# Second mixture of a fused attention and two-mixture kernel: router rounds cut into pieces, quarter additions reordered, one weight sum moved

## The chip, the cores and the metric

One core of a Trainium2 chip runs the whole kernel. The metric is the device time of one execution in microseconds (us). The kernel before took 1454.73 us, the median of 3 runs (1454.37 to 1455.91).

## The reference

Attention over clusters, then a gated feed-forward block, then a second mixture of eight experts whose weights per token come from a router that is balanced in eight rounds. Only the second mixture (`_moe2_ref`) is touched:

```python
N, D = x.shape                      # 1536 tokens, 512
E = w_gate.shape[1]                 # 8 experts, F = 1024
logits = x @ w_gate
logits = logits - logits.max()
P = np.exp(logits)
for _ in range(8):
    P /= P.sum(1, keepdims=True) + 1e-09
    P /= P.sum(0, keepdims=True) + 1e-09
    P *= N / E
out = np.zeros((N, D), dtype=np.float32)
for e in range(E):
    h = np.maximum(x @ w1[e], 0.0)
    ye = h @ w2[e]
    out += P[:, e:e + 1] * ye
```

## The kernel before

The second mixture is done in 16 sets (`s`), each half an expert's 1024 hidden columns. A set is two matrix products, each by the fast scheme that takes seven block products in place of eight, so it has 14 products, `i` = 0 to 13; `n` = 14 s + i. Products 0 to 6 make the hidden layer (PSUM tiles `a`), 7 to 13 the output layer (tiles `b`). Each float32 product is three matmuls of halves: a high part (`wfh`, `ah`, `xfh`, cast by ScalarE, written ACT below) and a low part (`wfl`, `al`, `xfl`, the difference, taken by VectorE, DVE). One block product of a layer is itself done by seven quarter products: `quad(s, q)` computes one into PSUM tile `q` (first layer's products 0 to 2) or `r` (`four=True`, for product 7), and `quad_add` lets DVE add it into the hidden block `h`. Quarters 1, 6, 7 and 4 share one PSUM bank (`QB`), so each waits until the one before it is added.

All four compute engines run an order that is written out by hand in one loop over `n`: what is written earlier is earlier on its engine's queue, and an instruction that waits holds up all behind it on that engine. At the top of a step come the operands for products one to three ahead (`factor` is `factor_hi` on ACT and `factor_lo` on DVE; `h_hi` and `h_lo` the same for hidden blocks; `h_s1` to `h_s4` sum hidden blocks on DVE) and the emptying of the product just done (`evacuate_a`, `evacuate_b`); then the matmuls of product `i`. In the output layer the products 1, 6, 7 and 4 (steps 7, 9, 11, 13) accumulate in one set of three PSUM banks, with a read by `evacuate_b` between them; the staging buffer of each read is a quarter of `acc1` (`RING` for the first seven).

`gate()` is a generator that computes the router's weights `Pg` on the side. The table `ROUNDS` says how many of its pieces are run at the end of which step (s, i). A round has two pieces: nine DVE instructions on the 128x12x8 weights, and one matmul `col` of the column sums `cs` against ones, which TensorE (PE) runs in its own order. Its results are first read when expert 1 starts (set 2, step 8). `w_t4` subtracts a weight sum in place (`ws`) for product 13 at step 11, just ahead of the cast of that sum. `x4_sums` and `x4_rest` make operands of the quarters of product 7 from the `x` that lies in `acc1`; set 0, steps 11 to 13, and set 1, products 1 and 2, hold them.

The lines of the profile that the prediction speaks of: L652 and L1041 are the products' matmuls, L1021 the quarters, L991 `col`, L747 DVE's sums (quarter additions are `h<-q` and `h<-r`), L750 its low parts, L1174 `h_s2`, L1074 and L1072 ACT's casts of hidden blocks, L863 its casts of weights, L1137, L1130 and L1116 the emptying of output products (ACT with weights, ACT without, DVE in the last set), L983 to L995 the router's rounds.

Of the kernel before, what the change touches and what calls it, by code (L numbers as in the profile page):

```python
# [8 lines left out]
F32 = mybir.dt.float32  # L9
# [8 lines left out]
P = 128  # L18
# [7 lines left out]
E = 8  # L26
# [12 lines left out]
def attention_moe_kernel(ctx, tc, kq, vp, cent, w_in, w_out, w_gate, w1, w2, out):  # L39
# [706 lines left out]
    def tt(e, out, in0, in1, op):  # L746
        e.tensor_tensor(out=out, in0=in0, in1=in1, op=op)  # L747
# [84 lines left out]
    def w_t4(n, e):  # L832
        _, _, b21, _, t = wst[n // 7]
        tt(e, t, b21, t, ALU.subtract)
# [105 lines left out]
    def gate():  # L940

        pair = ahp.tile([P, HT], F32, name="pair", tag="ah")
        first, lt = pair[:, :CH], pair[:, CH:]
        gps.memset(first[: P // 2], 0.0)
        ps = ps1.tile([P, 512], F32, name="gl", tag="g")[:, :CH]

        def logits(k0):
            for k in (k0, k0 + 1):
                for c in range(4):
                    nc.tensor.matmul(ps[CQ * c : CQ * (c + 1)], lhsT=wgr[:, k], rhs=acc1[:, k, c * CH : (c + 1) * CH], start=k == 0, stop=k == KC - 1, skip_group_check=True)  # L950

        logits(0)
        yield
        act.copy(first[P // 2 :], ps[: P // 2])
        yield
        logits(2)
        yield
        tt(vec, lt, ps, first, ALU.add)
        for _ in range(2):
            yield  # L960
        plog = ps1.tile([P, 512], F32, name="plog", tag="g")
        for t in range(CH // P):
            nc.tensor.transpose(plog[:, t * P : (t + 1) * P], lt[:, t * P : (t + 1) * P], ident)
        act.copy(Pg.rearrange("p (c t) e -> p c t e", c=4), plog[:, :CH].rearrange("p (t c x) -> p c t x", t=CH // P, c=4)[:, :, :, :E])
        mx = sk.tile([P, 4], F32, name="mx")
        vec.tensor_reduce(out=mx[:, 0:1], in_=Pg, axis=AX.XY, op=ALU.max)
        yield
        yield
        ps = ps1.tile([P, 512], F32, name="mxt", tag="g")
        nc.tensor.transpose(ps[:1, :P], mx[:, 0:1], ident)  # L970
        vec.tensor_reduce(out=mx[:1, 1:2], in_=ps[:1, :P], axis=AX.X, op=ALU.max, negate=True)
        yield
        yield
        ps = ps1.tile([P, 512], F32, name="mxb", tag="g")
        nc.tensor.matmul(ps[:, :1], lhsT=ones[:1, :], rhs=mx[:1, 1:2], start=True, stop=True)
        vec.tensor_copy(mx[:, 2:3], ps[:, :1])
        yield
        act.activation(Pg, Pg, AF.Exp, bias=mx[:, 2:3])
        rs = sk.tile([P, TT], F32, name="rs")
        cs = sk.tile([P, E], F32, name="cs")  # L980
        cr = sk.tile([P, E], F32, name="ccr")
        for it in range(8):
            vec.tensor_reduce(out=rs, in_=Pg, axis=AX.X, op=ALU.add)  # L983
            vec.tensor_scalar(out=rs, in0=rs, scalar1=1e-9, scalar2=None, op0=ALU.add)
            vec.reciprocal(rs, rs)
            tt(vec, Pg, Pg, rs.unsqueeze(2).to_broadcast([P, TT, E]), ALU.mult)
            vec.tensor_reduce(out=cs, in_=Pg.rearrange("p t e -> p e t"), axis=AX.X, op=ALU.add)
            yield
            yield
            ps = ps1.tile([P, 512], F32, name=f"col{it}", tag="g")  # L990
            nc.tensor.matmul(ps[:, :E], lhsT=ones, rhs=cs, start=True, stop=True)  # L991
            vec.tensor_scalar(out=cr, in0=ps[:, :E], scalar1=1e-9, scalar2=None, op0=ALU.add)
            vec.reciprocal(cr, cr)
            tt(vec, Pg, Pg, cr.unsqueeze(1).to_broadcast([P, TT, E]), ALU.mult)
            vec.tensor_scalar(out=Pg, in0=Pg, scalar1=float(NTOK // E), scalar2=None, op0=ALU.mult)  # L995


    sets = {}

# [95 lines left out]
        return to[i * HT : (i + 1) * HT, j * HD : (j + 1) * HD].rearrange("(t p) d -> p t d", p=P)  # L1095

    stages, stores = [0], [0]
    RING = (0, 1, 0, 1, 2, 0, 1)
    kept = {}

    def stage():
# [213 lines left out]
    nc.sync.dma_start(out=wgr[:, :, :E], in_=w_gate.rearrange("(k p) e -> p k e", p=P))  # L1315
    ones = sk.tile([P, P], F32, name="ones")
    gps.memset(ones, 1.0)
    Pg = sk.tile([P, TT, E], F32, name="Pg")

    gating = None  # L1320
    LATES = {7: 6, 8: 3, 9: 7, 10: 2, 11: 4}
    ROUNDS = {**{(0, i): 1 for i in range(14)}, (1, 2): 1, (1, 3): 2, (1, 4): 1, **{(1, i): 1 for i in range(10, 14)}, (2, 2): 1, (2, 3): 2, (2, 4): 2}
    acc2 = acc1.rearrange("p k (t d) -> p k t d", d=HD)
    ENG = mybir.EngineType
    with tc.manual_schedule(engines={ENG.PE, ENG.DVE, ENG.Activation, ENG.Pool}):
        psn = {}
        for n in range(14 * NS + 1):
# [3 lines left out]
            if late:  # L1331
                h_hi(s, late, 1, late == 2)
                h_lo(s, late, 1, late == 2)
            if i == 5:
                factor_hi(n + 3)
                if s == 0:
                    h_hi(s, 1, 0, relu=True)
                    h_hi(s, 1, 1, relu=True)
# [8 lines left out]
            if i == 0:  # L1347
                if s == 0:
                    x_quad_rest(2, 4)
                    t2 = h_block(0, "21")  # L1350
                    x_sum(t2, (1, 1), (0, 1))
                    x_factor(6, t2)
                else:
                    quad_factor(s)
                    factor(n + 2, vec)
                    w_sums2(n, vec)
                factor(n + 3, vec)
# [11 lines left out]
            if i == 3:  # L1369
                factor(n + 2, vec)  # L1370
                factor(n + 3, vec)
                if s:
                    quad_factor(s, True)
                w_load(n + 11)
                if s == 0:
                    x_sum((1, 0), (1, 0), t2)
                    x4_raw()
# [41 lines left out]
            if i in (8, 9):  # L1419
                factor(n + 2, vec)  # L1420
            if i in (10, 11, 12, 13):
                if i == 11:
                    w_t4(n - 4, vec)
                if i == 12:
                    w_load(n + 9)
                    w_sums1(n + 2, vec)
                factor(n + 2, vec)
                if i == 13:
                    quad_sums(s + 1)
                if s == 0:  # L1430
                    if i == 11:
                        x4_sums()
                    if i > 11:
                        x4_rest(i - 12)
            p = order(n)[i % 7]
            if i == 0:
                g = groups1(n, ready.pop(n), xf[1])
# [6 lines left out]
            elif i == 1:  # L1444
# [4 lines left out]
                multiply(psn[n + 1], g[1:2], False)  # L1449
                quad_add(s, 5)  # L1450
                quad_add(s, 6)
                if s == 1:
                    x4_rest(2)
                if s == 0:
                    x_sum((0, 0), t2, (0, 0), (0,))
            elif i == 2:
# [2 lines left out]
                quad(s, 3)  # L1459
                multiply(psn[n], g[3:], False)  # L1460
                quad_add(s, 7)
                if s == 1:
                    x4_rest(3)
                if s == 0:
                    x_sum((0, 0), t2, (0, 0), (1,))
                quad(s, 4)
                quad_add(s, 3)
                if s == 0:
                    x_factor(7, (0, 0), (0,))
                quad_add(s, 4)  # L1470
# [6 lines left out]
            elif i == 6:  # L1477
                if s == 0:
                    psn[n] = whole4(s, n)
            elif i < 7:  # L1480
                psn[n] = product(n, groups1(n, ready.pop(n), xf[p]))
            elif i == 7 and s:
                for q in (2, 1, 5):
                    quad(s, q, True)
                g = groups2([hf.pop((s, p, k)) for k in range(2)], ready.pop(n))
                psn[n] = sets[n // 7, 1] = [ps3.tile([P, 512], F32, name=f"b{s}_1_{u}", tag="s") for u in range(3)]
                opened = set()
                half_product(psn[n], g, 0, slice(0, 6), opened)
                quad_add(s, 2, True)
                quad_add(s, 1, True)  # L1490
                quad_add(s, 5, True)
                h_s1(s, (1,))
                h_hi(s, 5, 1)
                quad(s, 6, True)
                quad(s, 3, True)
                half_product(psn[n], g, 1, slice(0, 3), opened)
                quad_add(s, 6, True)
                h_lo(s, 5, 0)
                factor(n + 2, vec)
                quad_add(s, 3, True)  # L1500
                quad(s, 7, True)
                half_product(psn[n], g, 1, slice(3, 6), opened)
                quad_add(s, 7, True)
                h_lo(s, 5, 1)
                quad(s, 4, True)
                ready.pop(n - 1)
                h_s2(s, (0,))
                h_hi(s, 6, 0)
                quad_add(s, 4, True)
                h_s2(s, (1,))  # L1510
                h_lo(s, 6, 0)
            else:
                psn[n] = product(n, groups2([hf.pop((s, p, k)) for k in range(2)], ready.pop(n)), by_half=n < 14 * NS - 1)
            psn.pop(n - 3, None)
            if n == 0:
                gating = gate()
            if gating is not None:
                if s == 2 and i == 7:
                    for _ in gating:
                        pass  # L1520
                for _ in range(ROUNDS.get((s, i), 0)):
                    next(gating, None)


_OUTS = [((NTOK, DM), 'float32')]
# [35 lines left out]
```

## Time and profile before

| | |
|---|---|
| profiled execution, own time | 1453.9 us |
| its span, first to last instruction | 1452.1 us |
| median of 3 runs | 1454.73 us (1454.37 to 1455.91) |
| PE busy | 1432.2 us (99%) |
| DVE busy | 1207.1 us (83%) |
| ACT busy | 965.3 us (66%) |
| POOL busy | 367.3 us (25%) |
| granted clock of PE | 1.00 |
| span of the second mixture | from 486.5 us on |

The own time lies 1.8 us above the span and 0.8 us below the median of the runs. PE is busy in nearly all of the span, so time can be won only where its matmuls start later than the ones before them allow; the rows below show such places. A set takes 59.0 us.

### The profile page before, as it was taken

What the parts mean: (1) busy time and instruction counts of PE and PEld (TensorE: products, weight loads), DVE (VectorE), ACT (ScalarE), POOL (GpSimd) and SP (SyncE); (2) the same over time, 40 slices, a digit from 0 to 9 for tenths busy, and PEclk for the clock granted to TensorE, in tenths of its full rate; (3) what the DMA queues carried; (4) which work ended last, traced back from release to release, by engine and by line L of the source; (5) the groups of instructions that cost most, each with busy time, mean ns of one, the idle gap of its engine ahead of it and who ended that gap; (6) DMA issues with size and microseconds to landing.
All of it is one profiled execution on the core that took longest, in us unless ns stands there. A gap on an engine that the chain in (4) does not pass through costs nothing.

```text
span 1452.1 us, 25386 instructions
## 1 busy us (share of the span) xinstructions
PE 1432.2 (99%) x9703; PEld 1290.1 (89%) x9704; DVE 1207.1 (83%) x2045; ACT 965.3 (66%) x1848; POOL 367.3 (25%) x356
## 2 busy tenths in 40 slices
PE   8999999999999999999999999999999999999998
PEld 5777777888888898989999999999999999999997
DVE  7788888778787989997888878888788787887888
ACT  7677677654735476648767577676775876757764
POOL 6677653111120000201332222120211211202111
PEclk9999999999999999999999999999999999999999
DMA  7665621121130026657598797785956959659576
GB/s 211 183 178 147 183 65 45 58 73 59 58 102 29 3 95 144 111 100 175 114 199 131 145 192 119 155 133 94 196 93 118 159 88 176 112 100 181 87 147 131
DMA packets 136315, 177.49 MB, mean 122 GB/s; under 512 B 6273, under 2 KB 108673, under 8 KB 136193
## 3 DMA queue, kind: packets, MB, share of 16 engines
q0 software_dynamic: 83584, 87.30, 39.7%
q1 hardware_dynamic: 51104, 87.32, 19.5%
q8 instruction: 76, 1.25, 0.3%
q10 hardware_dynamic: 1504, 1.25, 0.3%
q14 instruction: 47, 0.38, 0.1%
HBM read 65.36 MB, written 88.87 MB: 106 GB/s over the span
## 4 chain that ended last, share of the span: by engine, by line
PE 71%; DVE 7%; ACT 3%; issue 2%; DVEq 0%; ACTq 0%
PE b L652 27%; PE a L652 20%; PE y L706 9%; PE q L1021 4%; PE b L1041 4%; PE r L1021 3%; PE l L652 3%; DVE h L747 1%; DVE wfl L750 1%; DVE acc L1116 1%; ACT h L674 1%; DVE h L678 1%; ACT acc L1137 0%; ACT gh L688 0%; ACT h L683 0%
## 5 line engine op out<-in xcount | busy, mean ns | idle before, releaser
L652 PE MATMUL b<-wfh,ah 128*128 128x256 f32 x1164 | 332.9, 286 | 2.8 <-DVE acc L1116 2.0
L652 PE MATMUL b<-wfl,ah 128*128 128x256 f32 x1164 | 329.1, 283 | 0.0
L652 PE MATMUL b<-wfh,al 128*128 128x256 f32 x1164 | 329.1, 283 | 0.0
L1146 POOL DMA_DIRECT2D out_dram<-acc x87 | 126.5, 1712 | 557.6 <-ACT acc L1137 460.5
L652 PEld LDWEIGHTS b<-wfh,ah 128*128 128x128 f32 x1164 | 222.7, 191 | 7.8 <-DVE h L747 2.9
L652 PEld LDWEIGHTS b<-wfl,ah 128*128 128x128 f32 x1164 | 222.9, 192 | 0.0
L652 PEld LDWEIGHTS b<-wfh,al 128*128 128x128 f32 x1164 | 222.9, 192 | 0.0
L652 PE MATMUL a<-xfh,wfh 128*128 128x512 f32 (+1 forms) x640 | 215.9, 337 | 0.1
L652 PE MATMUL a<-xfl,wfh 128*128 128x512 f32 (+1 forms) x640 | 215.8, 337 | 0.0
L652 PE MATMUL a<-xfh,wfl 128*128 128x512 f32 (+1 forms) x640 | 215.5, 337 | 0.0
L1074 ACT CAST ah<-h 128x768 fp32r<-128x768 f32 x160 | 135.1, 845 | 117.8 <-DVE h L1174 54.8
L1137 ACT ACTIVATE acc<-b,Pg 128x256 f32<-128x256 f32 x512 | 198.6, 505 | 0.0
L1061 ACT COPY h<-a 128x512 f32<-128x512 f32 x192 | 111.7, 603 | 109.5 <-PE a L652 99.7
L750 DVE TENSOR_TENSOR al<-h,ah 128x768 fp32r<-128x768 f32 x160 | 152.7, 955 | 11.0 <-ACT ah L1074 6.5
L652 PEld LDWEIGHTS a<-xfh,wfl 128*128 128x128 f32 x640 | 120.9, 189 | 12.9
L652 PEld LDWEIGHTS a<-xfh,wfh 128*128 128x128 f32 x640 | 121.1, 189 | 11.8 <-issue 0.6
L652 PEld LDWEIGHTS a<-xfl,wfh 128*128 128x128 f32 x640 | 121.1, 189 | 10.3
L313 ACT ACTIVATE p<-s,m 128x768 f32<-128x768 f32 x96 | 86.5, 902 | 39.5 <-DVE m L304 36.9
L304 DVE TENSOR_REDUCE m<-s 128x1 f32<-128x768 f32 x96 | 90.0, 951 | 13.5 <-PE s L297 13.1
L323 POOL TENSOR_SCALAR p<-p,rec 128x768 f32<-128x768 f32 x96 | 86.4, 912 | 49.1 <-DVE rec L318 40.1
L747 DVE TENSOR_TENSOR h<-q,h 128x384 f32<-128x384 f32 x112 | 61.9, 556 | 40.7 <-PE q L1021 38.7
L111 POOL TENSOR_TENSOR wr<-wr,u 128x512 f32<-128x512 f32 x32 | 44.2, 1383 | 183.2 <-DVE u L110 146.3
(260 smaller groups left out, 3402.6 us busy)
## 6 DMA issues: line engine op xcount, KB each, us to landing
out_dram<-acc POOLq DMA_DIRECT2D x91, 768.0 KB, 9.3
w0r<-in_w_dram SPq DMA_DIRECT2D x16, 1024.0 KB, 5.6
w1r<-in_w_dram SPq DMA_DIRECT2D x16, 1024.0 KB, 7.2
qk<-qk SPq DMA_DIRECT2D x45, 192.0 KB, 3.5
wr<-in_w_in_dram SPq DMA_DIRECT2D x16, 512.0 KB, 3.8
wr<-in_w_out_dram SPq DMA_DIRECT2D x16, 512.0 KB, 3.5
first_out<-acc POOLq DMA_DIRECT2D x10, 768.0 KB, 9.2
raw<-in_kq_dram SPq DMA_DIRECT2D x16, 384.0 KB, 4.4
```

What stands on the lines that cost most here:

```text
L304: nc.vector.tensor_reduce(out=m, in_=tiles[i]["s"][:, :S], axis=AX.X, op=ALU.max, negate=True)
L313: nc.scalar.activation(t["p"], t.pop("s")[:, :S], AF.Exp, bias=t.pop("m"), accum_out=chunks[c]["sum"][:, j, 0:1])
L323: nc.gpsimd.tensor_scalar(out=p, in0=p, scalar1=chunks[c]["rec"][:, j : j + 1], scalar2=1.0, op0=ALU.mult, op1=ALU.mult)
L652: nc.tensor.matmul(ps[u][:, cols], lhsT=lf(i, k), rhs=rt(j, k), start=fresh and u not in opened, stop=k == 1 and q == 2, skip_group_check= ...
L706: nc.tensor.matmul(out, lhsT=w[:, k, d * P : (d + 1) * P], rhs=g, start=first, stop=last, skip_group_check=True)
L747: e.tensor_tensor(out=out, in0=in0, in1=in1, op=op)
L750: e.tensor_tensor(out=lo, in0=x, in1=r(hi), op=ALU.subtract)
L1021: nc.tensor.matmul(ps, lhsT=quad_lhs(s, q, a, four), rhs=(x4 if four else xq)[b][:, XQ[q]], start=j == 0 and q in (1, 2, 5), stop=j == 2, ...
L1061: act.copy(bank(t, u), ps[u])
L1074: act.copy(hi, x)
L1137: act.mul(t[:, 2 * u + m], z[:, m], g)
L1146: gps.dma_start(out=to, in_=t, accum_op=ALU.add)
```

## The change

Six things. The router's weights lie in a tile with a ninth column that always holds 1e-9, so the row sums come out with that addend, and the factor N / E is part of the column factor: seven DVE instructions in a round in place of nine. A round has four pieces, and the pieces are spread anew: some between the quarter additions of products 1 and 2 of sets 1 and 2, three at a time at the top of steps 10 and 12 of set 1. In product 7 the last quarter's addition comes ahead of both `h_s2`, and the low part of the next weights after the addition of quarter 7. `w_t4` moves from step 11 to the top of step 10. `x4_sums` moves from step 11 to 12 of set 0, the four parts of `x4_rest` to set 0 step 13 (two), set 1 step 0 and step 3. In `RING` the fifth and sixth staging buffers change places.

```diff
         for it in range(8):
             vec.tensor_reduce(out=rs, in_=Pg, axis=AX.X, op=ALU.add)
-            vec.tensor_scalar(out=rs, in0=rs, scalar1=1e-9, scalar2=None, op0=ALU.add)
             vec.reciprocal(rs, rs)
-            tt(vec, Pg, Pg, rs.unsqueeze(2).to_broadcast([P, TT, E]), ALU.mult)
-            vec.tensor_reduce(out=cs, in_=Pg.rearrange("p t e -> p e t"), axis=AX.X, op=ALU.add)
-            yield
+            if it:
+                yield
+            tt(vec, shares, shares, rs.unsqueeze(2).to_broadcast([P, TT, E]), ALU.mult)
+            vec.tensor_reduce(out=cs, in_=shares.rearrange("p t e -> p e t"), axis=AX.X, op=ALU.add)
             yield
             ps = ps1.tile([P, 512], F32, name=f"col{it}", tag="g")
             nc.tensor.matmul(ps[:, :E], lhsT=ones, rhs=cs, start=True, stop=True)
-            vec.tensor_scalar(out=cr, in0=ps[:, :E], scalar1=1e-9, scalar2=None, op0=ALU.add)
+            yield
+            vec.tensor_scalar(out=cr, in0=ps[:, :E], scalar1=1e-9, scalar2=float(E / NTOK), op0=ALU.add, op1=ALU.mult)
             vec.reciprocal(cr, cr)
-            tt(vec, Pg, Pg, cr.unsqueeze(1).to_broadcast([P, TT, E]), ALU.mult)
-            vec.tensor_scalar(out=Pg, in0=Pg, scalar1=float(NTOK // E), scalar2=None, op0=ALU.mult)
-
+            tt(vec, shares, shares, cr.unsqueeze(1).to_broadcast([P, TT, E]), ALU.mult)
+            yield
+
+    def route(times):
+        for _ in range(times):
+            next(gating)
...
-    RING = (0, 1, 0, 1, 2, 0, 1)
+    RING = (0, 1, 0, 1, 0, 2, 1)
...
-    Pg = sk.tile([P, TT, E], F32, name="Pg")
+    Pg = sk.tile([P, TT, E + 1], F32, name="Pg")
+    shares = Pg[:, :, :E]
+    gps.memset(Pg, 1e-9)
...
-    ROUNDS = {**{(0, i): 1 for i in range(14)}, (1, 2): 1, (1, 3): 2, (1, 4): 1, **{(1, i): 1 for i in range(10, 14)}, (2, 2): 1, (2, 3): 2, (2, 4): 2}
+    ROUNDS = {**{(0, i): 1 for i in range(12)}, (0, 12): 3, (0, 13): 1, (1, 2): 1, (1, 3): 3, (1, 4): 1, (1, 10): 1, (1, 12): 1, (2, 2): 1, (2, 3): 3, (2, 4): 1, (2, 5): 1}
...
             if late:
                 h_hi(s, late, 1, late == 2)
                 h_lo(s, late, 1, late == 2)
+            if i == 10:
+                w_t4(n - 3, vec)
+            if s == 1 and i in (10, 12):
+                route(3)
...
-                if i == 11:
-                    w_t4(n - 4, vec)
...
-                if s == 0:
-                    if i == 11:
-                        x4_sums()
-                    if i > 11:
-                        x4_rest(i - 12)
+                if s == 0 and i == 12:
+                    x4_sums()
+                if s == 0 and i == 13:
+                    x4_rest(0, 1)
...
                 quad_add(s, 7)
-                if s == 1:
-                    x4_rest(3)
+                if 0 < s < 3:
+                    route(1)
...
                 quad_add(s, 3)
+                if 0 < s < 3:
+                    route(1)
...
                 quad_add(s, 6, True)
                 h_lo(s, 5, 0)
-                factor(n + 2, vec)
+                factor_hi(n + 2)
                 quad_add(s, 3, True)
                 quad(s, 7, True)
                 half_product(psn[n], g, 1, slice(3, 6), opened)
                 quad_add(s, 7, True)
+                factor_lo(n + 2, vec)
                 h_lo(s, 5, 1)
                 quad(s, 4, True)
                 ready.pop(n - 1)
+                quad_add(s, 4, True)
                 h_s2(s, (0,))
                 h_hi(s, 6, 0)
-                quad_add(s, 4, True)
                 h_s2(s, (1,))
                 h_lo(s, 6, 0)
```

Three places of the order. First, DVE in product 7 of set 3, which is the same in sets 1 to 15. Before (`h_3` with `r_` is a quarter addition, quarters 3, 7 and then 4; `wfl` the low part of the next weights):

```order
L750 TENSOR_TENSOR al_3_0_7847<-h_3_7656,ah_3_0_7787 128x768
L750 TENSOR_TENSOR wfl_7850<-ws_7653,wfh_7849 128x512
L747 TENSOR_TENSOR h_3_7748<-r_0_7792,h_3_7748 128x384
L747 TENSOR_TENSOR h_3_7748<-r_2_7794,h_3_7748 128x384
L750 TENSOR_TENSOR al_3_1_7867<-h_3_7656,ah_3_1_7829 128x768
L1174 SCALAR_TENSOR_TENSOR h_3_7593<-h_3_7593,h_3_7656 128x768
L747 TENSOR_TENSOR h_3_7748<-r_2_7794,h_3_7748 128x384
L1174 SCALAR_TENSOR_TENSOR h_3_7593<-h_3_7593,h_3_7656 128x768
```

And the same place now:

```order
L750 TENSOR_TENSOR al_3_0_7832<-h_3_7641,ah_3_0_7772 128x768
L747 TENSOR_TENSOR h_3_7733<-r_0_7777,h_3_7733 128x384
L747 TENSOR_TENSOR h_3_7733<-r_2_7779,h_3_7733 128x384
L750 TENSOR_TENSOR wfl_7835<-ws_7638,wfh_7834 128x512
L750 TENSOR_TENSOR al_3_1_7852<-h_3_7641,ah_3_1_7814 128x768
L747 TENSOR_TENSOR h_3_7733<-r_2_7779,h_3_7733 128x384
L1178 SCALAR_TENSOR_TENSOR h_3_7578<-h_3_7578,h_3_7641 128x768 x2
```

`wfl` went behind the additions of quarters 3 and 7, and the addition of quarter 4 went ahead of the first of the two `h_s2`.

Second, DVE in set 1, steps 10 and 11, before. `al_1_1_6607` is the second low part for product 11; the nine lines from `ccr` to `cs` are a round:

```order
L750 TENSOR_TENSOR al_1_1_6607<-h_1_6190,ah_1_1_6605 128x768
L1082 SCALAR_TENSOR_TENSOR al_1_0_6615<-h_1_6370,ah_1_0_6613 128x768
L750 TENSOR_TENSOR wfl_6618<-w1r_6024,wfh_6617 128x512
L992 TENSOR_SCALAR ccr<-col_6657 128x8
L993 RECIPROCAL ccr<-ccr 128x8
L747 TENSOR_TENSOR Pg<-Pg,ccr 128x96
L995 TENSOR_SCALAR Pg<-Pg 128x96
L983 TENSOR_REDUCE rs<-Pg 128x12
L984 TENSOR_SCALAR rs<-rs 128x12
L985 RECIPROCAL rs<-rs 128x12
L747 TENSOR_TENSOR Pg<-Pg,rs 128x96
L987 TENSOR_REDUCE cs<-Pg 128x8
```

And the same place now, with the weight sum `ws_6258` of `w_t4` behind the low part:

```order
L750 TENSOR_TENSOR al_1_1_6603<-h_1_6192,ah_1_1_6601 128x768
L747 TENSOR_TENSOR ws_6258<-w1r_6022,ws_6258 128x512
L993 TENSOR_SCALAR ccr<-col_6358 128x8
L994 RECIPROCAL ccr<-ccr 128x8
L747 TENSOR_TENSOR Pg<-Pg,ccr 128x12x8
L983 TENSOR_REDUCE rs<-Pg 128x12
L984 RECIPROCAL rs<-rs 128x12
L747 TENSOR_TENSOR Pg<-Pg,rs 128x12x8
L988 TENSOR_REDUCE cs<-Pg 128x8
L1086 SCALAR_TENSOR_TENSOR al_1_0_6619<-h_1_6366,ah_1_0_6617 128x768
```

Before, the round used the sum `col_6657` that PE makes at the end of product 10; now it uses one that PE made in step 4 (`col_6358`), and `cs` is made for the sum at the end of product 10.

Third, PE at the end of product 10 of set 1, now; before it stood at the same place, with another round's `cs`:

```order
L652 MATMUL b_5_2_6510<-wfh_6504,ah_1_1_6547 128x256
L652 MATMUL b_5_2_6510<-wfl_6505,ah_1_1_6547 128x256
L652 MATMUL b_5_2_6510<-wfh_6504,al_1_1_6549 128x256
L991 MATMUL col_6661<-cs,ones 128x8
L652 MATMUL b_1_0_6415<-wfh_6561,ah_1_0_6557 128x256
L652 MATMUL b_1_0_6415<-wfl_6562,ah_1_0_6557 128x256
```

`b_1_0_6415` is the first matmul of product 11; nothing on PE moved here, only what `col` waits for.

## Rows read from the trace of the kernel before

**Rows 1.** Waits of PE, whole span: who waited for whom, total us, times, longest.

```profile
PE r L1021 <- DVE h L747: 2.3, 4, 0.8
PE b L652 <- DVE acc L1116: 2.0, 2, 1.6
...
PE col L991 <- DVE cs L987: 0.9, 2, 0.4
PE b L652 <- ACT acc L1130: 0.8, 1, 0.8
...
PE q L1021 <- DVE h L747: 0.4, 1, 0.4
```

**Rows 2.** All waits in 689 to 1400 us, which is sets 3 to 14.

```profile
ACT wfh L863 <- DVE ws L747: 19.5, 12, 1.6
...
PEld b L652 <- DVE h L747: 2.3, 12, 0.2
```

**Rows 3.** Timeline of PE in set 3: start, us, instruction.

```profile
707.99 0.34 PE L1021 MATMUL r<-x4h,wql 128*128 128x384 f32 x1
...
709.25 0.44 PE L1021 MATMUL r<-x4h,wfh 128*128 128x384 f32 x1
...
711.07 0.28 PE L652 MATMUL b<-wfl,ah 128*128 128x256 f32 x1
711.19 0.28 PE L652 MATMUL b<-wfh,al 128*128 128x256 f32 x1
711.46 0.39 PE L652 MATMUL b<-wfh,ah 128*128 128x256 f32 x1
711.68 0.28 PE L652 MATMUL b<-wfl,ah 128*128 128x256 f32 x1
...
731.59 0.28 PE L652 MATMUL b<-wfh,al 128*128 128x256 f32 x1
731.79 0.38 PE L652 MATMUL b<-wfh,ah 128*128 128x256 f32 x1
```

**Rows 4.** Timeline of DVE in product 7 of set 3.

```profile
707.59 0.68 DVE L750 TENSOR_TENSOR wfl<-ws,wfh 128x512 fp32r<-128x512 f32 x1
708.19 1.02 DVE L747 TENSOR_TENSOR h<-r,h 128x384 f32<-128x384 f32 x2
709.12 0.95 DVE L750 TENSOR_TENSOR al<-h,ah 128x768 fp32r<-128x768 f32 x1
709.98 0.95 DVE L1174 SCALAR_TENSOR_TENSOR h<-h,h 128x768 f32<-128x768 f32 x1
710.85 0.55 DVE L747 TENSOR_TENSOR h<-r,h 128x384 f32<-128x384 f32 x1
711.32 0.95 DVE L1174 SCALAR_TENSOR_TENSOR h<-h,h 128x768 f32<-128x768 f32 x1
```

**Rows 5.** Timeline of ACT in set 3; in brackets idle time before, and what ended it.

```profile
712.38 0.84 ACT L1074 CAST ah<-h 128x768 fp32r<-128x768 f32 x1 [0.50 <-PE b L652]
713.12 2.29 ACT L1137 ACTIVATE acc<-b,Pg 128x256 f32<-128x256 f32 x6
...
729.65 0.62 ACT L863 CAST wfh<-ws 128x512 fp32r<-128x512 f32 x1 [1.63 <-DVE ws L747]
```

**Rows 6.** Timeline of DVE in set 1, steps 10 and 11: a low part, a round's ends.

```profile
599.89 0.95 DVE L750 TENSOR_TENSOR al<-h,ah 128x768 fp32r<-128x768 f32 x1
...
603.34 0.16 DVE L992 TENSOR_SCALAR ccr<-col 128x8 f32<-128x8 f32 x1
...
605.36 0.35 DVE L987 TENSOR_REDUCE cs<-Pg 128x8 f32<-128x96 f32 x1
```

**Rows 7.** Timeline of PE at the end of product 10 of set 1.

```profile
601.16 0.29 PE L991 MATMUL col<-cs,ones 128*128 128x8 f32 x2
```

**Rows 8.** Timeline of PE in set 2, first quarters of product 7.

```profile
640.40 0.39 PE L652 MATMUL a<-xfh,wfl 128*128 128x512 f32 x1
640.92 0.44 PE L1021 MATMUL r<-x4h,wfh 128*128 128x384 f32 x1
```

**Rows 9.** Timeline of DVE in the last set, step 11.

```profile
1439.78 0.69 DVE L750 TENSOR_TENSOR wfl<-ws,wfh 128x512 fp32r<-128x512 f32 x1 [0.69 <-ACT wfh L863]
```

More of the change, by code (lines that the diff above doesn't have):

```diff
@@ L963, in gate @@
             nc.tensor.transpose(plog[:, t * P : (t + 1) * P], lt[:, t * P : (t + 1) * P], ident)
-        act.copy(Pg.rearrange("p (c t) e -> p c t e", c=4), plog[:, :CH].rearrange("p (t c x) -> p c t x", t=CH // P, c=4)[:, :, :, :E])
+        act.copy(shares.rearrange("p (c t) e -> p c t e", c=4), plog[:, :CH].rearrange("p (t c x) -> p c t x", t=CH // P, c=4)[:, :, :, :E])
         mx = sk.tile([P, 4], F32, name="mx")
-        vec.tensor_reduce(out=mx[:, 0:1], in_=Pg, axis=AX.XY, op=ALU.max)
+        vec.tensor_reduce(out=mx[:, 0:1], in_=shares, axis=AX.XY, op=ALU.max)
         yield
@@ L977, in gate @@
         yield
-        act.activation(Pg, Pg, AF.Exp, bias=mx[:, 2:3])
+        act.activation(shares, shares, AF.Exp, bias=mx[:, 2:3])
         rs = sk.tile([P, TT], F32, name="rs")
@@ L1353, in attention_moe_kernel @@
                 else:
+                    if s == 1:
+                        x4_rest(2)
                     quad_factor(s)
@@ L1374, in attention_moe_kernel @@
                 w_load(n + 11)
+                if s == 1:
+                    x4_rest(3)
                 if s == 0:
@@ L1451, in attention_moe_kernel @@
                 quad_add(s, 6)
-                if s == 1:
-                    x4_rest(2)
+                if 0 < s < 3:
+                    route(1)
                 if s == 0:
@@ L1461, in attention_moe_kernel @@
                 quad_add(s, 7)
-                if s == 1:
-                    x4_rest(3)
+                if 0 < s < 3:
+                    route(1)
                 if s == 0:
@@ L1467, in attention_moe_kernel @@
                 quad_add(s, 3)
+                if 0 < s < 3:
+                    route(1)
                 if s == 0:
@@ L1516, in attention_moe_kernel @@
                 gating = gate()
[L1517 to L1522, printed above, removed]
+            route(ROUNDS.get((s, i), 0))
 _OUTS = [((NTOK, DM), 'float32')]
```

## The prediction

> **What bounds the kernel now.** I read the page first (the table above): PE is busy almost throughout at its full granted clock, the other engines are not. So a step counts only if a matmul starts earlier or later by it, and the next view is the list of PE's own waits over the span [rows 1]. It is short. Four waits of quarter matmuls (`r`) for DVE's additions, one of `q`, two of the router's `col` for DVE's column sums and one of an output product for ACT's emptying all lie in sets 0 to 2, where the router runs. Two more, 2.0 us together, are in the last set, where DVE empties PSUM.
>
> That list leaves out waits too short to show as idle time, because a matmul's modelled end overlaps the next start. So I looked at sets 3 to 14 by start times. The list for all engines there has twelve waits of weight loads for a DVE addition, one a set, and twelve of ACT's cast for DVE's weight sum [rows 2]. In set 3 they look like this [rows 3]. Matmuls of width 256 start 0.12 us apart (711.07, 711.19), but then 0.27 and 0.22 pass: 0.25 us lost, as the product's third PSUM bank is still held by quarter 4's addition, which ends at 710.85 + 0.55 = 711.40 [rows 4]. A matmul that had to wait is also 0.10 longer than its kind (0.39 against 0.28), and the next starts that much later. By the same mark the first matmul of quarter 4 waited (0.44 against 0.34): about 0.12. The third place is the start of product 13: 0.20 in place of 0.12, and 0.38 long: 0.18. So a late set loses 0.25 + 0.12 + 0.18 = 0.55 us. And an idle time w in the list of waits costs PE w + 0.16 (the 0.28 of the matmul before, less its step of 0.12) + 0.10.
>
> **The change part by part.** Each is costed at the place where PE meets it; against the profile's own time of 1453.9 us.
>
> *Quarter additions in product 7, sets 1 to 15.* Now the additions of quarters 3 and 7 come ahead of `wfl`. Steps of DVE, start to start [rows 4]: `wfl` 0.60, an addition 0.465 (two in 0.93), `al` 0.86, `h_s2` 0.87. Quarter 7's last matmul ends at 707.99 + 0.34 = 708.33 [rows 3], so its addition runs from 708.37 to 708.92 (0.04 is also what passed between the addition's end at 709.21 and PE's start at 709.25). Quarter 4's weight load was due near 709.12, so the 0.12 goes. Then `wfl` at 708.83, `al` at 709.43, quarter 4's addition 710.29 to 710.84; the bank is asked for near 711.06. So the 0.25 goes, with some 0.2 to spare.
>
> What is late next: the second `h_s2` ends at 710.76 + 0.87 + 0.95 = 712.58 in place of 712.27. ACT's second cast of product 9's operand follows `h_s2` by 0.11 (712.27 to 712.38 in [rows 5]), so it starts at 712.69, and the emptying of product 7, queued behind it, at 713.43 in place of 713.12. PE may add product 9 to that set of banks only when a bank's two pieces are read: pieces start 0.36 apart and last about 0.5 (six in 2.29), so the first bank is free at 713.43 + 0.36 + 0.50 + 0.04 = 714.33. Product 9's natural start was 711.68 + 23 x 0.12 = 714.44, now 0.37 earlier, 714.07. PE waits 0.26 and 0.10 there: 0.36 of 0.37 is given back. This new wait rests on a sum of nine steps, so it may be off by 0.3: I keep 0 and 0.72 as its bounds.
>
> Here a rule speaks against the reorder. The additions start 0.465 apart and last 0.55 [rows 4]. The Trainium skill, VectorE: DVE Perf Modes, section "The DRAIN you can't avoid", says that the next instruction does not start until the pipe is empty. By that rule each of the moved steps would take its whole duration, quarter 4's addition would end near 711.1, after it is asked for, and a late set would lose about 0.2 us rather than win; the sum would come out some 5 us smaller. By the rows it does not.
>
> *The weight sum `w_t4` at step 10.* DVE does it in a stretch in which it waits for ACT's next cast anyway, behind the low parts for product 11. ACT's cast no longer idles 1.63 us for it [rows 5], so the emptying of product 11 moves up by more than the 0.18 that product 13 waited: the 0.18 goes. If that cover were gone it would be 0.60 on DVE, still ahead of nothing that PE asks for then. Net for a late set: 0.55 - 0.36 = 0.19; twelve sets (3 to 14): **-2.3 us**.
>
> In the last set DVE's own queue sets the end: `w_t4` (0.68) and the wait of 0.69 behind it [rows 9] stood between two emptyings of PSUM. Both go, 1.37, less the 0.31 by which ACT's run is later: **-1.1**.
>
> *Set 0.* `x4_sums` on DVE no longer stands ahead of ACT's emptying of product 11, since that now goes to buffer 0; its earlier store was issued two products before, the same distance at which the third buffer was reused without a wait. PE's wait of 0.8 for ACT [rows 1] goes: **-0.9** with its tail. Below nothing: if the store were late, the wait would only stay. The memset of `Pg` on POOL is one more, long before anything reads it.
>
> *Set 1, quarter 7 of product 2.* The `q` wait (0.4, so 0.66) is DVE's backlog out of set 0. DVE is ahead by half a round and the weight sum's wait, but all three early `x4_rest` now lie before it, and PE arrives 0.7 earlier: I leave 0.2 of it. **-0.5** (bounds 0 and -0.66).
>
> *The router's rounds.* Nine instructions take 603.34 to 605.36 + 0.35, 2.37 us [rows 6]; seven at the same mean 1.84. No trace shows the strided nine-column form; it reads as many elements, so from 1.8 to the 2.37 of nine. Between the quarter additions of products 1 and 2 the pieces fall where DVE waits for PE. The `col` behind product 2 needs column sums that end some 0.15 after PE is ready; the two waits of 0.9 together, 1.4 with tails, become two of 0.25: **-0.9**. Without 2.3 us of round before steps 3 and 4, DVE reaches product 7 of sets 1 and 2 nearly as early as in later sets. So the four `r` waits (2.3 + 4 x 0.26 = 3.3), the bank wait (2 x 0.25), the one at 640.92 (0.52 less 0.23, and 0.10: 0.4 [rows 8]) and 0.18 in set 2 go, 4.4 in all, against the new wait at product 9 (0.36 and, with ACT's shorter copies in set 1, about 0.2): **-3.8**.
>
> *The new order at step 10 of set 1.* Here the change adds a wait. The `col` at the end of product 10 needed sums made long before; it comes up at 601.16 [rows 7]. Now its sums are made behind the low part that ends at 600.84 [rows 6], `w_t4` (0.60) and seven round instructions (1.84): ready at 600.76 + 2.44 + 0.06 = 603.3, 2.1 late, and 0.3 later still as this stretch now follows the later `h_s2`. Queued behind it on PE is all of product 11. **+2.4**, bounds 1.8 and 2.9; nothing lets DVE come 2 us earlier here, since its low parts follow ACT's casts. At step 12 the same layout costs nothing: that `col` comes a product and this wait later, while DVE has caught up.
>
> Sum: -2.3 - 1.1 - 0.9 - 0.5 - 0.9 - 3.8 + 2.4 = -7.1, so 1446.8 for a run like the profiled one. That one lay 0.8 below the median of the runs shown; I put the median at **1447.5**.
>
> **The rivals.**
> *No new wait at product 9.* ACT's emptying comes in time after all, because a step in my nine is shorter. For: 0.26 is little over nine steps. Against: before, that bank was free only 0.4 ahead of need (713.12 + 0.36 + 0.50 + 0.04 against 714.44), and both ends move by more than 0.3. Twelve sets win 0.36 more, sets 1 and 2 0.56: 1442.6.
> *No change.* The wait at product 9 is twice as long: late sets lose 0.17 in place of winning 0.19, 4.3 us less, and set 2 0.4 less: 1452.2.
> *Slower.* ACT empties products 7, 8 and 9 in one run with casts between; if its delay passes on to products 10 and 11, PE waits three times a set. For: PE's 36 x 0.12 = 4.3 us a product is no more than what ACT needs for one: 6 x 0.36, two casts of 0.74 (712.38 to 713.12) and one of weights, 0.6, are 4.2 [rows 5]. Against: that delay is 0.31 and does not grow by itself, and PE, having waited at product 9, is no earlier than before at products 10 and 11, where it did not wait. At 0.5 each a late set loses 1.5 - 0.55 = 0.95: 11.4 lost in place of 2.3 won, and 2 in sets 1 and 2: 1463.2. It decides, past +0.2%, from a loss of about 0.6 a set.
> *The clock.* After the 2.4 us wait of PE its clock could fall to the lower level, 1.2 GHz, and product 11 take 8.6 in place of 36 x 0.12 = 4.3: 1451.8. Against: the longest wait now is 1.6 [rows 1], with a granted clock of 1.00 over the span. The Trainium skill, TensorE: Matmul & The Clock Gate, "Part 1: The HAM clock gate", says that an idle engine's clock is halved; the trace has no idle time as long as this one to show it.
> *The reorder does nothing.* If the late sets neither won nor lost: 1449.8; this lies inside the forecast.
>
> **How the numbers follow.** Forecast 0.55 (1444.5 to 1450); no wait at product 9 0.20; no change 0.13; slower 0.06; the clock 0.02; larger gains 0.04. A range of 1442.0 to 1452.0 leaves out about 2 in 10. This kernel's measurement can tell 0.2%, 2.9 us: faster 0.82, same 0.11, slower 0.07.
>
> **What would show it.** Right: sets 3 to 14 at about 58.8 us; no wait of weight loads for quarter additions; in its place a matmul 0.10 too long at the start of product 9, behind ACT's L1137 or its like; a single PE wait for `cs` of about 2.2 at the end of product 10 of set 1; none for the emptying of product 11 in set 0; in the last set 1.1 us less behind product 12. Wrong: sets at 58.4 (no wait at product 9) or above 59.0 (ACT passes it on), or no wait at that `col`, which would take away the one loss in the sum.

## The result, and the profile after

The changed kernel takes 1463.97 us (median of 5 runs, 1462.61 to 1468.47) beside 1454.73 (5 runs, 1454.17 to 1456.09): a ratio of 1.0068, with a 95% interval of 1.005 to 1.0087. It is slower; the forecast was 1447.5.

Two things in the trace of after answer at once. The head of the list of PE's waits from 500 us on, which answers to [rows 1], shows that what was to go did go: the four `r` waits, the two of 0.4 for `cs` and the one for ACT in set 0. The 2.6 for `cs` is the new wait at the `col`. But there are 17 waits of `q` for quarter additions, where there was one:

```profile
PE q L1025 <- DVE h L747: 7.3, 17, 0.5
PE col L991 <- DVE cs L988: 2.6, 1, 2.6
PE b L652 <- DVE acc L1120: 0.7, 1, 0.7
```

The list of all waits in 689 to 1410 us, which answers to [rows 2], names an engine that was not in the sum at all, the DMA:

```profile
ACT acc L1141 <- DMA out_dram<-acc: 29.9, 11, 3.5
...
DVE wql L750 <- ACT wqh L818: 45.9, 12, 4.6
...
PEld q L1025 <- DVE h L747: 16.8, 23, 0.9
```

In the list of before, over 689 to 1400 us, ACT waited for no DMA, and the wait of `wql` was a quarter of this:

```profile
DVE wql L750 <- ACT wqh L818: 11.5, 12, 1.0
```

The starts of the first matmul of each set, read off the timeline of PE, put the 10.06 us between the two spans in their places (in us; the last column is experiment e5, below):

| stretch | before | changed | e5 |
|---|---|---|---|
| up to set 1 | 551.93 | 552.02 | 550.32 |
| set 1 | 62.64 | 64.06 | 59.64 |
| set 2 | 62.65 | 59.48 | 59.55 |
| sets 3 to 14 | 708.23 | 718.17 | 705.82 |
| last set, to its last matmul | 61.49 | 61.81 | 60.38 |
| from there to the end | 5.19 | 6.65 | 6.66 |

In "up to set 1", the changed kernel is 0.87 behind already at the first matmul of set 0 (486.53 and 487.40). That belongs to the execution and not to the change: its granted clock was 0.50 from 12.2 to 19.0 us, where that of before was 1.00, and e5, with the same code up to there, starts set 0 at 485.69. Set 0 itself won 0.77 (65.39 to 64.62). Set 3 takes 58.82, just as forecast. From set 4 on a set takes 59.5 to 60.8.

The timelines of DVE, SP's queue (`SPq`, which issues the loads), ACT, DVE and PE in sets 3 and 4 show how a set loses it:

```profile
721.45 0.68 DVE L747 TENSOR_TENSOR ws<-w1r,ws 128x512 f32<-128x512 f32 x1
...
724.15 0.69 DVE L750 TENSOR_TENSOR wfl<-w1r,wfh 128x512 fp32r<-128x512 f32 x1
...
724.87 0.37 SPq L757 DMA_DIRECT2D w1r<-in_w_dram  x1
...
734.95 2.30 ACT L1141 ACTIVATE acc<-b,Pg 128x256 f32<-128x256 f32 x6 [2.34 <-DMA out_dram<-acc]
737.10 0.65 ACT L818 CAST wqh<-qs 128x512 fp32r<-128x512 f32 x1
...
737.78 0.69 DVE L750 TENSOR_TENSOR wql<-qs,wqh 128x512 fp32r<-128x512 f32 x1 [3.39 <-ACT wqh L818]
...
744.06 0.44 PE L1025 MATMUL q<-xqh,wqh 128*128 128x384 f32 x1 [0.47 <-DVE h L747]
```

And the timelines of DVE and SP of before, at the same place:

```profile
728.93 0.69 DVE L747 TENSOR_TENSOR ws<-w1r,ws 128x512 f32<-128x512 f32 x1
...
729.68 0.37 SPq L757 DMA_DIRECT2D w1r<-in_w_dram  x1
```

Before, `w_t4` (`ws<-w1r`) was the last reader of the raw output weights `w1r`; the 1 MB load of the next ones into that buffer started as it ended. With `w_t4` moved up, the last reader is a `wfl` at 724.15, and the load starts at 724.87. Counted from the first matmul of its set that is 49.31 in place of 52.46 us, 3.15 earlier. It is 1.9 us behind POOL's accumulating store of product 9, where it was 5.4 behind it. The landing of that one store, before:

```profile
L1146 POOL DMA_DIRECT2D out_dram<-acc x1: 1431/1431/1431, 724.3 to 724.3; - x1
...
DMA to landing us min/median/max: 8.9/8.9/8.9
```

and after:

```profile
L1150 POOL DMA_DIRECT2D out_dram<-acc x1: 1431/1431/1431, 723.0 to 723.0; - x1
...
DMA to landing us min/median/max: 11.9/11.9/11.9
```

So the store lands at about 734.8. Emptied products go round four staging buffers, so product 13 is emptied into the one that product 9's store reads. ACT starts that at 734.95, after 2.34 idle. Relative to the start of the next set, `wqh` is now cast 2.72 us behind it, where it was 1.44; behind that cast DVE's `wql` and its next quarter additions are as late, and quarter 7 of the next set, which shares its bank with quarter 6, waits 0.47: 0.73 us with the 0.16 and 0.10 that the prediction adds to a wait (its tail). In some sets quarter 6 waits too.

The DMA was busy already with stores alone. In the changed kernel, product 8's store was still under way when product 9's was issued:

```profile
718.60 1.45 POOL L1150 DMA_DIRECT2D out_dram<-acc  x1 [2.70 <-ACT acc L1141]
```

It landed 9.7 us later, at 728.3. Before the load, from 723.0 to 724.9, the busy times by windows end with a DMA share (the time of the packets over that of 16 engines) of 1.23, at 198 GB/s, and all of these packets are the stores':

```profile
723.00:724.90 1.90, 1.90 (x18) 1.90 (x17) 1.62 (x3) 1.90 (x5) 1.39 (x1) 1.00 1.23 198
```

In the kernel before, the load was issued 0.7 us after product 8's store had landed (issued at 719.94, landed at 729.01). The Trainium skill, DMA: Bandwidth & Descriptors, section "Issuing engines are not separate DMA queues", says that transfers issued by SP and by GpSimd run on the same 16 engines and interleave; this trace agrees, with 8.9 and 11.9 us for the same 768 KB.

The second loss is in set 1. The busy times by windows of 601.0 to 608.0, around the new `col`; the column behind the engines is the granted clock:

```profile
601.00:602.70 1.70, 1.61 (x13) 1.61 (x14) 1.70 (x4) 1.30 (x3) 0.00 (x0) 0.99 1.27 191
602.70:606.00 3.30, 3.30 (x18) 3.30 (x17) 1.50 (x2) 1.35 (x2) 0.00 (x0) 0.50 1.19 175
606.00:608.00 2.00, 2.00 (x18) 2.00 (x18) 0.73 (x2) 0.64 (x1) 0.00 (x0) 0.98 1.13 303
```

PE stood from about 598.50 to 601.09, worked 1.6 us at full clock, and then 3.3 us at the lower level, 0.50 of 2.4 GHz. Some 15 matmuls start 0.21 apart in place of 0.12: 1.4 us.

### The profile page after: what moved, and what is told of

The parts are those of the page before. It is cut to its first block, busy times and chain, and to the rows that moved or that the text cites. A ratio compares the mean times of both kernels' runs of the same rounds, so it can differ in the third digit from the quotient of the medians.

```text
span 1462.2 us, 25367 instructions
## 1 busy us (share of the span) xinstructions
PE 1434.3 (98%) x9703; PEld 1290.0 (88%) x9704; DVE 1201.0 (82%) x2029; ACT 965.6 (66%) x1848; POOL 363.7 (25%) x357
## 4 chain that ended last, share of the span: by engine, by line
PE 53%; DVE 10%; ACT 8%; DMA 8%; issue 3%; ACTq 0%; DVEq 0%
PE a L652 17%; PE b L652 14%; PE y L706 9%; DMA out_dram<-acc 8%; ACT acc L1141 3%; PE b L1045 3%; PE r L1025 3%; PE l L652 3%; PE q L1025 3%; DVE h L747 3%; ACT ah L1078 2%; DVE wfl L750 2%; DVE al L750 1%; DVE w0r L747 1%; DVE h L1178 1%
```

## The experiments

**Holding the load alone (e1).** In the changed kernel VectorE copies one column of the weights onto itself at step 11, where the sum stood:

```
             if i in (10, 11, 12, 13):
+                if i == 11:
+                    first = wst[(n - 4) // 7][2][:, 0, :1]
+                    vec.tensor_copy(first, first)
```

> The changed kernel, in which VectorE copies one column of the raw output weights onto itself at step 11, where the weight sum stood before. Nothing moves back; the only effect meant is that the buffer of the weights comes free about 3 us later, and so the 1 MB load into it is issued about 3 us later (4.7 us behind the store of product 9 in place of 1.9). Theory A (the early load delays that store, and ScalarE's emptying of product 13 waits for it): the store lands in about 9.3 us in place of 12, ScalarE's wait of 2.3 to 3.5 shrinks under 0.6, no quarter matmul waits at the start of the next set, sets 4 to 14 take 58.8 in place of 59.5 to 60.8: 1463.97 - 12.3 - 1.0 = 1450.7. Theory B (the order of VectorE's or ScalarE's own work is to blame, the store is late by itself): no change, 1464.

Measured 1451.22, ratio to before (1454.51 on this chip, for e1 to e4) 0.9979 (0.9969 to 0.9988). The load starts at 729.19, 4.9 behind the store, which lands in 8.7:

```profile
L1150 POOL DMA_DIRECT2D out_dram<-acc x1: 1431/1431/1431, 724.3 to 724.3; - x1
...
DMA to landing us min/median/max: 8.7/8.7/8.7
```

Sets 3 to 14 take 58.82 each, and ACT's 11 waits for stores in them are one:

```profile
ACT acc L1141 <- DMA out_dram<-acc: 1.2, 1, 1.2
```

Theory A holds. There was a surprise that speaks for it too: set 1 became 2.3 longer. In set 0 the unheld load had run ahead of the stores (issued at 539.59); held, it was issued at 543.29, among the stores of products 10 to 12. Their landing there, in the changed kernel:

```profile
L1150 POOL DMA_DIRECT2D first_out<-acc x3: 1431/1446/1538, 542.6 to 551.1; - x3
...
DMA to landing us min/median/max: 8.2/9.0/9.6
```

and with the load held:

```profile
L1150 POOL DMA_DIRECT2D first_out<-acc x3: 1431/1446/1538, 541.7 to 550.2; - x3
...
DMA to landing us min/median/max: 11.8/12.3/12.7
```

On ACT's timeline the emptying of product 13, into the buffer of product 10, then waits for it:

```profile
553.63 1.07 ACT L1134 COPY acc<-b 128x512 f32<-128x512 f32 x2 [2.37 <-DMA first_out<-acc]
```

So one edit took the collision out of the late sets and put the same one into set 0, with the same wait behind it.

**The weight sum alone (e2).** Before, with `w_t4(n - 3, vec)` at the top of step 10 in place of `w_t4(n - 4, vec)` at step 11:

```
+            if i == 10:
+                w_t4(n - 3, vec)
...
-                if i == 11:
-                    w_t4(n - 4, vec)
```

> The kernel before with the weight sum at step 10 alone, without the rest. Theory A (early load): the load is issued some 4 us earlier, the store of product 9 lands about 3 us later, ScalarE waits 1.5 to 3 us for it, quarter matmuls of the next set wait: late sets 59.0 - 0.18 + 0.73 = 59.55, about 12 sets, so some 6 us more: 1461 (1459 to 1463). Theory B (order of the other parts): the weight sum alone wins the 0.18 of product 13, 12 sets and the tail of 1.1: 1451.5.

Measured 1461.14, ratio 1.0046 (1.0031 to 1.0061). In sets 3 to 14 ACT's waits for stores are there without any other part of the change:

```profile
ACT acc L1137 <- DMA out_dram<-acc: 26.4, 10, 3.5
```

Where none came before it, a set takes 58.82 (the sets that start at 676.43 and 1093.58): the 0.18 of product 13 is real. The others take up to 60.35. This one line accounts for the sign of the result.

**The `col` later (e3).** The changed kernel, with two entries of the table of rounds changed:

```
-    ROUNDS = {... (1, 10): 1, (1, 12): 1, ...}
+    ROUNDS = {... (1, 11): 1, (1, 13): 1, ...}
```

> The changed kernel with the two col matmuls of the router in set 1 that stand behind products 10 and 12 put behind products 11 and 13. Theory A: PE's wait of 2.6 (2.75 with its tail) goes, and with it the stretch of product 11 at half clock (15 starts of 0.21 in place of 0.12, 1.4 us): set 1 takes 59.9 in place of 64.06, the time is 4.2 less, 1459.8. Theory B, the low clock has another cause: 2.75 less, 1461.2. Theory C, the wait moves to the new place: 1464.

Measured 1459.02, ratio 1.0037 (1.0024 to 1.005). Set 1 takes 59.64 in place of 64.06, 4.42 less, and in 600 to 606 us the clock stays up:

```profile
600.00:606.00 6.00, 6.00 (x52) 6.00 (x51) 5.83 (x13) 6.00 (x12) 0.60 (x1) 1.00 1.23 192
```

So the wait brought the low clock along. Theory A. The kernel of e1, which keeps the wait (2.60), has the low clock again: 0.50 from 604.0 to 607.3.

**The reorder alone (e4).** Before, with product 7 as changed:

```
-                factor(n + 2, vec)
+                factor_hi(n + 2)
                 quad_add(s, 3, True)
...
                 quad_add(s, 7, True)
+                factor_lo(n + 2, vec)
                 h_lo(s, 5, 1)
                 quad(s, 4, True)
                 ready.pop(n - 1)
+                quad_add(s, 4, True)
                 h_s2(s, (0,))
                 h_hi(s, 6, 0)
-                quad_add(s, 4, True)
```

> The kernel before with the new order of quarter additions in product 7 alone. Prediction on record: removes 0.25 + 0.12 and gives back 0.36 at product 9, so a late set stays at 59.0 and the time at 1454.5. If no wait came at product 9, sets of 58.63 and 14 x 0.37 less: 1449.6. If the additions had to wait for the end of each instruction before them, sets of 59.2 and 1457.

Measured 1457.78, ratio 1.0025 (1.0015 to 1.0035), a miss by 3.3: late sets take 59.33. That is the time the third case gave, but not its mechanism: in the changed kernel, as in the rows, an addition leaves room for its successor after 0.47 (708.64 to 709.11), not after its 0.55, and the bank wait is gone. The loss is at product 13, on the timeline of PE:

```profile
730.65 0.28 PE L652 MATMUL b<-wfh,al 128*128 128x256 f32 x1
731.16 0.39 PE L652 MATMUL b<-wfh,ah 128*128 128x256 f32 x1 [0.23 <-ACT acc L1137]
```

It waits 0.23 + 0.16 + 0.10 = 0.49 where it waited 0.18 [rows 3], since ACT's run is 0.31 later and still stands 1.6 for the weight sum. The reorder needs the early weight sum.

**Both mends (e5).** The changed kernel with the held load from set 1 on (`if i == 11 and s:`) and the later `col`.

> The changed kernel with both mends: the held load, from set 1 on only (in set 0 the same hold pushed the load under a store of the first set, which took 11.8 us in place of 8.2, and quarter matmuls of set 1 waited), and the two col matmuls behind products 11 and 13. If the two losses are separate: set 1 59.6, set 2 59.5, sets 3 to 14 58.82 and the tail of the held run, 1444.8 (1444 to 1446). If the mends hide one loss in the other, less is won: 1447.

Measured 1443.98, ratio to before (1453.71 there, for e5 to e8) 0.9933 (0.9918 to 0.9948). PE's waits from 500 us on are one line:

```profile
PE b L652 <- DVE acc L1120: 0.7, 1, 0.7
```

The two losses are separate. Against the kernel before on the same chip this one wins 9.7 us, where the forecast won 7.2 with a loss of 2.4 at the `col` in it, so the other terms come out right together. Part of that is luck: sets 1 and 2 won 0.9 more than forecast, and 0.84 was there before set 0 began (485.69 for 486.53), while 1.5 at the very end was not in the sum.

**Without the reorder (e6).** As e5, with product 7 as before.

> The same with product 7 in its old order (quarter 4's addition behind the first h_s2, the low part of the weights ahead of quarter 3's). If the reorder gives back at product 9 what it takes from quarter 4 and the bank (0.37 against 0.36), late sets stay at 58.82 and only sets 1 and 2 lose the second r wait, 0.66 each: 1446.1. If the reorder is worth its 0.37 somewhere, sets of 59.2 and 1450.

Measured 1444.92, ratio 0.9939 (0.9923 to 0.9956). Late sets take 58.82, like e5's: what the reorder takes it gives back. The second `r` waits do not return (sets 1 and 2 take 59.91 and 59.54), so that part of the expectation was wrong.

**Quarter 4's addition alone (e7).** As e5, with `factor(n + 2, vec)` in its old place and only the addition ahead of both `h_s2`:

```
-                factor_hi(n + 2)
+                factor(n + 2, vec)
                 quad_add(s, 3, True)
...
-                factor_lo(n + 2, vec)
```

> The same as both mended, but of the reorder only quarter 4's addition is moved ahead of both h_s2; the low part of the weights stays ahead of quarter 3's addition, so that VectorE does not idle before quarter 7. Theory: the bank wait of 0.25 goes, quarter 4's load wait of 0.12 stays, the second h_s2 ends where it ended before, so ScalarE's emptying of product 7 is not later and product 9 does not wait: late sets 59.0 - 0.25 - 0.18 = 58.57, 12 x 0.25 less than with both mended, and 0.66 twice more in sets 1 and 2: 1443.1. Rival: product 9 waits all the same, since any earlier start is given back there: 58.82 and 1446.

Measured 1441.26, ratio 0.9911 (0.9897 to 0.9926). Eleven of sets 3 to 14 take 58.61 or 58.62, one 58.70. It beats both kernels, and product 9 does not wait in it: moving `wfl` behind quarter 7's addition had left DVE idle for 0.22 ahead of that addition, and made `h_s2` and ACT late.

**The router part alone (e8).** As e3, with product 7 and the weight sum as before.

> The router part alone (rounds of seven, pieces between the quarter additions, earlier fourth-block work, the ring), with the two col matmuls behind products 11 and 13; product 7 and the weight sum as before. By the terms on record: set 0 0.9, the q wait 0.5, the col waits 0.9, the four r waits 3.3 less: 1449.1, with late sets at 59.0. Rival: the r waits come from product 7's own order and stay: 1452.4.

Measured 1448.87, ratio 0.9966 (0.9953 to 0.9979), late sets at 59.0. All four `r` waits go by the router part. Set 0 was a miss: expected 0.9 shorter, it takes 65.85 for 65.39. ACT's wait there is gone, but a `col` now waits for its sums, 1.26 with the tail:

```profile
PE col L991 <- DVE cs L988: 1.0, 1, 1.0
```

With the weight sum at step 10 (e6) that wait is not there, and set 0 takes 64.62. Sets 1 and 2 won 5.5 for the 4.7 expected, and this execution began set 0 0.78 earlier, so the total fits in part by luck.

## Why the prediction was wrong

**The step that failed** is "The weight sum `w_t4` at step 10". It looked for what DVE and ACT do with the moved sum, called it covered, and did not follow the buffer that the sum reads: its reader's end is what lets SP issue the next load. That load, 3.15 us earlier in its set, made product 9's store land in 11.9 us for 8.9; ACT waited 2.3 to 3.5 for it, and the next set's quarters came late. Its term in the late sets, -2.3, came out as 718.17 - 708.23 = +9.9. With the load held it is -2.4 (e5), so the rest of the term was sized rightly. In the last set -1.1 came out as +1.8: two late quarters (0.71 and 0.73), and 1.5 at the very end, below.

**The new `col` wait** was right in place and cause. The wait is 2.59 + 0.16 = 2.75 in place of 2.4, inside its bounds; the seven instructions took 599.14 to 600.71 + 0.32, 1.89 us for the 1.84 assumed. But the rival "The clock" came true with it, at 1.4 us and not the 4.3 of a whole product at half clock, since only 3.3 us ran slow. The Trainium skill, TensorE: Matmul & The Clock Gate, "Part 1: The HAM clock gate", says that idleness halves the clock; the granted 0.50 after this wait agrees. Set 1 lost 4.4 there in place of 2.4.

**What held.** The new wait at product 9 came where and as large as forecast, on the timeline of PE of the changed kernel: 0.27 and 0.10 above the step of 0.12, for 0.26 and 0.10 worked out:

```profile
712.28 0.28 PE L652 MATMUL b<-wfh,al 128*128 128x256 f32 x1
712.67 0.39 PE L652 MATMUL b<-wfh,ah 128*128 128x256 f32 x1
```

Undisturbed sets take 58.82 against "about 58.8". Set 0 won 0.77 for 0.9, but the reason given is not the only one: with the weight sum alone (e2), `x4_sums` and the ring as before, ACT's wait is gone too and set 0 takes 64.48, 0.91 less. Sets 1 and 2 won 3.0 + 3.1 = 6.1 without the `col` wait (e5) for 0.5 + 0.9 + 3.8 = 5.2: the `q` and `col` waits went altogether. The sums of DVE's steps were good to 0.1 us; e4 shows where adding parts was not: there the reorder's later ACT and the late weight sum meet.

**The rule weighed** against the rows in the reorder, from the Trainium skill, VectorE: DVE Perf Modes, "The DRAIN you can't avoid", would have made the late sets 0.2 slower; by e1 and e5 they are 0.18 faster, and the steps of 0.47 are shorter than the 0.55 of an addition. The same section also says that a next operation that is not held starts earlier, which the prediction left out. **The slower rival** had the right time (1463.2) for a wrong reason: ACT passed nothing on through products 10 and 11.

**The end.** PE's last matmul came 1.1 earlier in e5's last set, as forecast, but the last stores then landed later. SP issues five of the ten; the landing is that of all ten. Here those of before,

```profile
L1121 SPq DMA_DIRECT2D out_dram<-acc x5: 345/373/384, 1443.1 to 1448.6; - x5
...
DMA to landing us min/median/max: 2.7/2.8/3.4
```

and those of the changed kernel,

```profile
L1125 SPq DMA_DIRECT2D out_dram<-acc x5: 372/383/783, 1451.7 to 1457.2; - x5
...
DMA to landing us min/median/max: 3.7/4.0/4.6
```

In the kernels with the early weight sum the last stores take 3.8 to 4.3 at the median (e1: 3.8, e2: 4.1, e5: 4.3), in e8 without it 2.6. The first of them is now issued 4.4 us behind the first of POOL's three accumulating stores of the last set and not 5.9. That these slow them is possible, but no run parted the two, and the stores issued after POOL's had landed (at 1455.1) are late too: 3.8 to 4.1, where those of before took 2.7 to 2.8. The cause stays open.

## What to carry to other kernels

An instruction that is moved earlier also frees what it reads earlier: for each operand of a moved step, ask which transfer waits for that buffer, and what that transfer will then run beside. Holding a buffer with a tiny late reader is a cheap way to test this, and here to mend it, but a hold that helps in one stretch can make the same collision in another. And a new wait of TensorE may cost more than its length: here 2.75 us took 1.4 of slow matmuls with it.

## What was not expected of the hardware

Alone, an accumulating store of 768 KB lands in 7.6 us (issued at 699.09 in the kernel before, with no other transfer beside it). Such stores alone keep the DMA's share at 1.2 with under 200 GB/s moved (723.0 to 724.9), and the second of two that overlap landed in 8.9 before the change. The 1 MB load made that 11.9 when it started 1.9 us behind the second store, 3.5 before the first had landed; it cost nothing to speak of when it started 4.9 behind (8.7 in e1), 0.3 after the first had landed (728.9). The distance to the one store does not decide this by itself. In set 0 of the kernel before, the load started 2.1 us behind product 10's store, with no other store under way, and that store landed in 8.9, only 1.3 over its time alone:

```profile
541.80 1.54 POOL L1146 DMA_DIRECT2D first_out<-acc  x1 [54.35 <-DVE al L1082]
...
543.89 0.37 SPq L757 DMA_DIRECT2D w1r<-in_w_dram  x1
```

So it is likely that the second store under way makes the load dear; no run changed that alone.

The clock was not low on the first matmuls after the wait: PE resumed at 601.09 at 0.99 of full speed, and the slow stretch stands from 602.7 to 606.0, inside product 11 with PE busy throughout.
